# Attention, SoLU-MoE and softplus-MoE on one core: sums transposed as four columns and repeated by DMAs, the first q in two pieces, new numbers for the list schedule

## The chip, the core and the metric

The kernel runs on one core of a Trainium2 chip. The metric is the device time of one execution in microseconds (us). A core has a matrix engine (TensorE, PE in the rows; its weight loads are PEld), VectorE (DVE), ScalarE (ACT), GpSimd (POOL, hardly used here) and SyncE (SP), which issues transfers; the engines run beside each other, each in the order of its own instructions, and wait for one another by semaphores. Matrix products land in PSUM, everything else lives in SBUF; DRAM is reached by transfers (DMA).

## What is computed

```python
scores = scale * np.matmul(q, k.transpose(0, 1, 3, 2))      # 4 batches, 8 heads, 576 x 64
thresh = np.max(scores, axis=-1, keepdims=True) - tau
scores = np.where(scores >= thresh, scores, -1e9)
attn = np.exp(scores - np.max(scores, axis=-1, keepdims=True))
attn = attn / (np.sum(attn, axis=-1, keepdims=True) + 1e-09)
x = (attn @ v) -> (2304, 512)
h = x @ w_in                     # 512 x 1024
solu = h * softmax(h)
x = layernorm(solu) * g_ln @ w_out          # 1024 x 512
h = x @ w2_in                    # 512 x 2048
out = softplus(h) @ w2_out       # 2048 x 512
```

## The kernel before

Attention works on pairs of heads that lie on the upper and lower 64 partitions. A score block (L393) is four products of 128 query rows by 288 keys; its two halves fill the two score buffers in PSUM, so the next block can't start before both have been read. On each half VectorE takes the row maximum (L349), ScalarE the exponential (L350), VectorE the mask, with the row sums as a by-product (L352). TensorE then transposes the masked scores against an identity (L368), ScalarE copies the result to SBUF (L371), and TensorE multiplies by v (L429). An item is one pair of heads with one or two such query blocks; there are 36 of them, 8 with one block and 28 with two, and 8 items for the rest of 64 rows that divide by their sums in another way.

The product has the queries along its free dimension, and so the reciprocals of the sums, which come out with queries on partitions (L357, L358, a tile `rinv` of 128 x 2 or 4), have to be turned too. Before, ScalarE repeats each of the columns 64 times (`rb`, L402), TensorE transposes the 128 x 128 that this makes (L408, one for each block), ScalarE copies the outcome (`x`, L410), and VectorE multiplies the product by it (L432).

The transposed attention output goes through the first MoE in units of 256 rows (L567 to L635) and is stored to DRAM (`x2s`); from there blocks of 512 rows go through the second MoE (L678, L701). The weights come as float64 words, and VectorE and ScalarE make two parts of each, high and low (L488 to L515): this preparation of `w_in` and `w_out` falls in the start, between the first attention items. Products of four banks of PSUM, the tag `w`, are shared by everything that isn't a score block.

A planner sets the order of all of it. Every operation is entered with an engine, a duration (`occ`, `fin`), what it waits for, the buffers that it takes, and a due time from tables of numbers (`JT`, `JA`, `LO`, `LAGS`, `LD`, `JIT`, `PREP` and others). `Plan.order` is a list scheduler: it runs the durations through a model of the engines, the transfers and TensorE's clock, and takes among the operations ready on an engine the one that is due first; `AHEAD` is how many ns it lets an engine wait for one due earlier. The program then stands in the order of the modelled starts. Where the model leaves TensorE idle early on, it puts in filler products of the identity (L288).

Of the kernel before, what the change touches and what calls it, by code (L numbers as in the profile page):

```python
# [9 lines left out]
F32 = mybir.dt.float32  # L10
# [12 lines left out]
P = 128  # L23
# [56 lines left out]
WARM = 130e3  # L80

# [7 lines left out]
class Plan:  # L89
# [17 lines left out]
    def order(self):  # L107
# [12 lines left out]
        mode, dma, done = "", 0, []  # L120
        win, work, slow = 0, {}, False
# [31 lines left out]
        while any(cand.values()):  # L153
# [62 lines left out]
def tile_attention_solu_softplus(ctx: ExitStack, tc: tile.TileContext, q, k, v, tau, w_in, w_out, g_ln, w2_in, w2_out, out):  # L216
# [22 lines left out]
    done = plan_of(nc, ctx, sb, const, ident, minus, pools, stacks, w1t, x2s, q, k, v, tau, w_in, w_out, g_ln, w2_in, w2_out, out).order()  # L239
# [24 lines left out]
def plan_of(nc, ctx, sb, const, ident, minus, pools, stacks, w1t, x2s, q, k, v, tau, w_in, w_out, g_ln, w2_in, w2_out, out):  # L264
# [5 lines left out]
    plan = Plan(dict(w=W_, s=S_, h2=4, E=NE, T=2, eT=NET, x=2, xr=NXR, xrT=1, q=NPAIR, k=NPAIR, v=NPAIR, ln=3, u=2,  # L270
# [28 lines left out]
    o_minus = op("ACT", 200, 300, lambda: act.activation(out=minus, in_=ident, func=AF.Copy, scale=-1.0), after=[o_ident], due=-60)  # L299
    o_table = op("ACT", 1300, 1300, lambda: act.preload_act_table_set("natural_log_exp_and_others"), due=-49.5)  # L300

    def queue(what, i):
        return "ACT" if f"{what}{i}" in ON_ACT else "SP"

    def load_qk(p, due):
# [4 lines left out]
        z["kq"], ql = [], []  # L310
# [66 lines left out]
    def item(n):  # L377
# [4 lines left out]
        sums = buf("at", "sums", f"sums{n}", [P, 4], bufs=4)  # L382
        E = [buf("at", "E", f"E{n}_{i}", [P, 1152], bufs=NE) for i in range(nt)]
        masks = {}
        for kk, i in enumerate(ts):
# [8 lines left out]
            sc = op("PE", 970, 1128, emit_s, after=z["kq"] + [z["scaled"]], takes=s, uses=[z["q"], z["k"]], due=j + JIT[n], mode="R")  # L394
# [6 lines left out]
        rb = buf("at", "rb", f"rb{n}", [P, 4, 64])  # L401
# [459 lines left out]
```

## Time and profile before

| | |
|---|---|
| median of 3 runs | 911.1 us (910.85 to 911.49) |
| profiled execution, its own time | 914.37 us |
| its span, first to last instruction | 912.6 us |
| mean granted clock of TensorE | 0.996 |
| TensorE busy | 899.6 us of the span |
| VectorE, ScalarE busy | 690.4, 591.1 us |
| transfers | 64.63 MB, mean 71 GB/s |

The profiled execution takes 1.8 us beside its span and lies 3.3 us above the median of the other runs. Matrix products overlap in the engine's pipe, so a busy time holds a modelled end; spacings between the starts of products tell more than their mean durations.

### The profile page before, as it was taken

How to read it: one execution, taken by the hardware profiler on the slowest of the kernel's cores; microseconds unless marked ns; L12 is line 12 of the kernel's file. 1: busy time of each engine (PE TensorE's matmuls, PEld its weight loads, DVE VectorE, ACT ScalarE, POOL GpSimd, SP SyncE). 2: the span in 40 equal slices, each digit the busy share in tenths (PEclk: the TensorE clock that was granted, in tenths of full speed). 3: DMA queues.
4: the chain of work that ended last, by engine and by line, in shares of the span. 5: the costliest groups of instructions: out<-in, count | busy, mean ns of one | idle time of the engine just before them, and what ended most of it. 6: DMA issues, size and time to landing. Idle time of an engine off the chain costs nothing.

```text
span 912.6 us, 14433 instructions
## 1 busy us (share of the span) xinstructions
PE 899.6 (99%) x5458; PEld 709.6 (78%) x5458; DVE 690.4 (76%) x1474; ACT 591.1 (65%) x1159; POOL 0.7 (0%) x6
## 2 busy tenths in 40 slices
PE   8999999999999999999999999999999999999998
PEld 6576676677677677788888878888888888888897
DVE  5999898898777778599958969985556555655565
ACT  6978887997778687676757746764444444444454
POOL 0000000000000000000000000000000000000000
PEclk9999999999999999999999999999999999999999
DMA  9405110230231000164414223430021001100010
GB/s 281 161 1 175 54 30 1 84 83 24 66 109 62 2 1 12 59 219 162 139 59 162 93 98 110 135 119 24 1 92 47 1 1 47 47 0 1 1 47 24
DMA packets 32052, 64.63 MB, mean 71 GB/s; under 512 B 3440, under 2 KB 12912, under 8 KB 31984
## 3 DMA queue, kind: packets, MB, share of 16 engines
q1 hardware_dynamic: 31104, 61.62, 20.8%
q10 hardware_dynamic: 880, 2.10, 0.8%
q8 instruction: 43, 0.70, 0.3%
q14 instruction: 25, 0.20, 0.1%
HBM read 49.55 MB, written 14.16 MB: 70 GB/s over the span
## 4 chain that ended last, share of the span: by engine, by line
PE 83%; DVE 7%; ACT 4%; DMA 4%; issue 1%; SPq 1%; ACTq 0%; DVEq 0%
PE w L701 21%; PE h L678 20%; PE w L567 8%; PE w L368 7%; PE w L429 6%; PE s L393 6%; PE w L627 6%; PE w L628 3%; PE w L610 1%; PE w L472 1%; DMA raw<-in_w_in_dram 1%; DVE E L352 1%; DVE nm L349 1%; PE s L450 1%; DMA q<-in_q_dram 1%
## 5 line engine op out<-in xcount | busy, mean ns | idle before, releaser
L678 PE MATMUL h<-x2m,w2h 128*128 128x512 f32 (+1 forms) x640 | 181.6, 368 | 0.0
L678 PEld LDWEIGHTS h<-x2m,w2h 128*128 128x128 f32 x640 | 116.5, 188 | 21.0
L349 DVE TENSOR_REDUCE nm<-s 128x1 f32<-128x576 f32 x144 | 102.7, 752 | 21.7 <-PE s L393 19.1
L678 PE MATMUL h<-x2m,w2l 128*128 128x512 f32 (+1 forms) x320 | 117.7, 368 | 0.0
L701 PE MATMUL w<-wo2h,gh 128*128 128x512 f32 x288 | 112.9, 392 | 1.1 <-ACT wo2h L503 1.1
L701 PE MATMUL w<-wo2l,gh 128*128 128x512 f32 x288 | 113.0, 393 | 0.6 <-DVE wo2l L505 0.6
L352 DVE SCALAR_TENSOR_TENSOR E<-E,etau 128x576 f32<-128x576 f32 x128 | 101.1, 815 | 16.3 <-ACT E L350 14.9
L701 PE MATMUL w<-wo2h,gl 128*128 128x512 f32 x288 | 112.7, 391 | 0.0
L371 ACT COPY eT<-w 128x512 f32<-128x512 f32 (+1 forms) x188 | 92.9, 554 | 19.5 <-PE w L368 18.9
L689 ACT ACTIVATE t<-h 128x512 f32<-128x512 f32 (+1 forms) x80 | 44.3, 554 | 90.9 <-PE h L678 90.9
L627 PE MATMUL w<-lhl,wo1h 128*128 128x512 f32 x288 | 102.8, 397 | 0.0
L350 ACT ACTIVATE E<-s,nm 128x576 f32<-128x576 f32 x128 | 91.6, 756 | 11.2 <-DVE nm L349 11.0
L691 DVE TENSOR_SCALAR gw<-t 128x512 f32<-128x512 f32 (+1 forms) x80 | 31.8, 399 | 80.3 <-ACT t L690 80.1
L693 ACT ACTIVATE gw<-gw 128x512 f32<-128x512 f32 (+1 forms) x80 | 47.1, 589 | 61.1 <-DVE t L692 60.0
L393 PE MATMUL s<-k,q 64*128 64x288 f32 x512 | 83.9, 429 | 2.0 <-ACT E L350 1.4
L628 PE MATMUL w<-lhl,wo1l 128*128 128x256 f32 x288 | 80.7, 280 | 0.0
L429 PE MATMUL w<-eT,v 128*64 128x256 f32 (+1 forms) x720 | 77.8, 364 | 1.6 <-ACT eT L371 1.5
L368 PE MATMUL w<-ident,E 128*128 128x128 f32 x576 | 78.4, 279 | 0.0
L368 PEld LDWEIGHTS w<-ident,E 128*128 128x128 f32 x576 | 63.6, 141 | 17.4 <-issue 6.4
L694 DVE SCALAR_TENSOR_TENSOR gw<-h,gw 128x512 f32<-128x512 f32 (+1 forms) x80 | 51.0, 637 | 33.1 <-ACT gw L693 32.0
L429 PEld LDWEIGHTS w<-eT,v 128*64 128x64 f32 x720 | 47.1, 138 | 28.0 <-ACT eT L371 4.4
L678 PEld LDWEIGHTS h<-x2m,w2l 128*128 128x128 f32 x320 | 60.3, 188 | 10.1
(107 smaller groups left out, 1573.2 us busy)
## 6 DMA issues: line engine op xcount, KB each, us to landing
x2s<-x SPq DMA_DIRECT2D x36, 256.0 KB, 2.0
x2m<-x2s SPq DMA_DIRECT2D x18, 512.0 KB, 6.0
raw_in<-in_w_in_dram SPq DMA_DIRECT2D x16, 512.0 KB, 3.8
raw_out<-in_w_out_dram SPq DMA_DIRECT2D x16, 512.0 KB, 3.6
v<-in_v_dram SPq DMA_DIRECT2D x15, 320.0 KB, 3.4
q<-in_q_dram SPq DMA_DIRECT2D x28, 144.0 KB, 3.6
out_dram<-yo SPq DMA_DIRECT2D x15, 256.0 KB, 2.1
raw<-in_w_out_dram SPq DMA_DIRECT2D x3, 1024.0 KB, 7.8
```

Of the source, the lines that this page charges most:

```text
L349: mx = op("DVE", 668, 750, lambda: dve.tensor_reduce(out=nm.t, in_=src(), axis=AX.XY, op=ALU.max, negate=True), after=[after], takes=[nm], ...
L350: ex = op("ACT", 638, 741, lambda: act.activation(out=dst().rearrange("p (a b) -> p a b", a=2), in_=src(), func=AF.Exp, bias=nm.t, scale=1.0),
L352: return op("DVE", 739, 900, lambda: dve.scalar_tensor_tensor(out=dst(), in0=dst(), scalar=etau, in1=dst(), op0=ALU.is_ge, op1=ALU.mult, a ...
L368: pe.transpose(bk.t[:, P * i:P * i + P], b_.t[:, c:c + P], ident)
L371: copies.append(op("ACT", occ, occ + 111, lambda: act.copy(out=eT.t[:, 0:width], in_=bk.t[:, 0:width]), after=[g], uses=[bk, eT], due=due))
L393: pe.matmul(s[h].t[:, nh, 0:288], z["q"].t[r, c:c + P], z["k"].t[r, 288 * nh:288 * nh + 288], start=True, stop=True)
L429: pe.matmul(o_.t[64 * h:64 * h + 64, 0:W], z["v"].t[:, vcols(c, h)], e[8 if c == 8 else 4 * h + c](), start=(i == 0), stop=(i == 4))
L567: pe.matmul(ps.t, x__[:, part, :], w_[:, part, 512 * n:512 * n + 512], start=(part == 0 and j_ == 0), stop=(part == 3 and j_ == 2))
L627: pe.matmul(o.t.rearrange("p (a q) -> p a q", a=2), w1t["wo1h"][:, c, P * m:P * m + P], lhl.t[:, :, c, :], start=(c == 0), stop=False)
L628: pe.matmul(o.t[:, 0:256], w1t["wo1l"][:, c, P * m:P * m + P], lhl.t[:, 0, c, :], start=False, stop=(c == 7))
L678: pe.matmul(ps.t[:, 0:n], w2t["in", a, c][:, part, :], x.t[:, b_, part, 0:n], start=(part == 0 and j_ == 0), stop=(part == 3 and j_ == 2))
L701: pe.matmul(ys[j].t, g_.t[:, P * j:P * j + P], w2t["out", a, c], start=(c == 0 and i == 0), stop=(c == NC2 - 1 and i == 2))
```

## The change

The reciprocals, two or four columns of `rinv`, are transposed as they are (L412 of the new file), to 2 or 4 partitions of 128 queries. ScalarE copies these rows (`r4`, L413), a transfer writes them to a small DRAM buffer `rs`, and two further transfers read them back, each row repeated over 64 partitions, into `x`. The first pair's q is loaded and scaled in two pieces, columns 0 to 191 and the rest. The multiplication moves from L432 to L437. The durations that the planner is told of are changed in many places, its transfer model starts at 2500 ns and its clock model slow, and every table of due times has new numbers.

```diff
-JT = [0.34, 7.73, 0.9, -3.39, 0.54, 0.49, 0.42, 9.02, 0.11, 3.15, -3.13, -0.51, -5.45, 1.01, 1.21, 6.91, -4.6, 8.15, -0.49, -0.88, -1.72, -3.81, 4.75, 9.79, 2.6, 9.72, 9.11, -5.74, -0.21, 2.17, 6.22, 2.62, -2.76, -1.92, 0.89, -0.0, -0.65, 0.66, -0.91, -2.44, -7.92, -1.24, -0.04, -1.57]
+JT = [11.45, 5.07, 3.31, 9.75, -11.65, 3.47, -0.64, -1.63, -10.27, 1.59, -2.28, 3.3, 9.05, 4.22, 9.97, -7.59, 4.34, -11.96, 7.76, 0.13, 0.83, 21.82, 2.41, 10.51, 14.94, -3.8, 1.84, -8.57, 4.79, -4.06, -8.32, -0.54, 0.33, -3.15, -15.82, 8.18, 2.14, 4.06, -0.76, 0.02, -5.72, -14.29, -0.14, 3.14]
...
-AHEAD = dict(PE=0, DVE=0, ACT=0, SP=20, POOL=20, X=20)
+AHEAD = dict(PE=35, DVE=100, ACT=10, SP=500, POOL=20, X=20)
...
+FIRST = 2500
...
-        mode, dma, done = "", 0, []
-        win, work, slow = 0, {}, False
+        mode, dma, done = "", FIRST, []
+        win, work, slow = 0, {}, True
...
-                o.end = dma + 1900
+                o.end = dma + 1900 + (o.fin or 0)
...
+    rs = [dram.tile([4, P], F32, tag=f"rs{n}", name=f"rs{n}") for n in range(len(items_of()))]
...
-        for h in range(2):
-            r = slice(64 * h, 64 * h + 64)
-            ql.append(load(queue("q", p), lambda r=r: q_.t[r, :], lambda h=h: q[p][:, 640 * h:640 * h + 576], 144, takes=() if h else [q_], uses=[q_] if h else (), due=due))
-        z["scaled"] = op("ACT", 574, 678, lambda: act.activation(out=q_.t, in_=q_.t, func=AF.Copy, scale=0.125), after=ql, uses=[q_], due=due + 0.5)
+        cuts = [0, 192, S] if p == 0 else [0, S]
+        z["scaled"] = []
+        for a, e in zip(cuts, cuts[1:]):
+            ql = []
+            for h in range(2):
+                r = slice(64 * h, 64 * h + 64)
+                tk = a == h == 0
+                ql.append(load(queue("q", p) if a == 0 else "SP", lambda r=r, a=a, e=e: q_.t[r, a:e], lambda h=h, a=a, e=e: q[p][:, 640 * h + a:640 * h + e], (e - a) / 4, takes=[q_] if tk else (), uses=() if tk else [q_], due=due + (1 if a else 0)))
+            occ = 110 + 0.806 * (e - a)
+            z["scaled"].append(op("ACT", occ, occ + 104, lambda a=a, e=e: act.activation(out=q_.t[:, a:e], in_=q_.t[:, a:e], func=AF.Copy, scale=0.125), after=ql, uses=[q_], due=due + 0.5))
...
-            sc = op("PE", 970, 1128, emit_s, after=z["kq"] + [z["scaled"]], takes=s, uses=[z["q"], z["k"]], due=j + JIT[n], mode="R")
+            sc = op("PE", 970, 1128, emit_s, after=z["kq"] + z["scaled"][0:1 if i == 0 else 2], takes=s, uses=[z["q"], z["k"]], due=j + JIT[n], mode="R")
...
-        rb = buf("at", "rb", f"rb{n}", [P, 4, 64])
-        o3 = op("ACT", 187 if nt == 1 else 310, 298 if nt == 1 else 410, lambda: act.copy(out=rb.t[:, 0:w, :], in_=rv.t[:, 0:w].unsqueeze(2).to_broadcast([P, w, 64])), after=[o2], takes=[rb], uses=[rv], due=jl + D_SUM)
         rbk = bank()
+        r4 = buf("at", "r4", f"r4{n}", [4, P], bufs=2)
         x = buf("at", "x", f"x{n}", [P, 256], bufs=2)
-
-        def emit_r():
-            for i in range(nt):
-                pe.transpose(rbk.t[:, P * i:P * i + P], rb.t[:, 2 * i:2 * i + 2, :].rearrange("p a b -> p (a b)"), ident)
-        rg = op("PE", 109 * nt, 109 * nt + 163, emit_r, after=[o3, o_ident], takes=[rbk, x], uses=[rb], due=jl + D_X, mode="T")
-        xc = op("ACT", 162 if nt == 1 else 263, 270 if nt == 1 else 395, lambda: act.copy(out=x.t[:, 0:W], in_=rbk.t[:, 0:W]), after=[rg], uses=[rbk, x], due=jl + D_X)
+        rg = op("PE", 64, 227, lambda: pe.transpose(rbk.t[0:w, 0:P], rv.t[:, 0:w], ident), after=[o2, o_ident], takes=[rbk], uses=[rv], due=jl + D_X, mode="T")
+        rc = op("ACT", 160, 265, lambda: act.copy(out=r4.t[0:w, :], in_=rbk.t[0:w, 0:P]), after=[rg], takes=[r4], uses=[rbk], due=jl + D_X)
+        wr = load("SP", lambda: rs[n][0:w], lambda: r4.t[0:w, :], 1, after=[rc], uses=[r4], due=jl + D_SUM)
+        xc = [load("SP", lambda h=h: x.t[64 * h:64 * h + 64, 0:W].rearrange("p (i q) -> p i q", q=P), lambda h=h: bass.AP(tensor=rs[n].tensor, offset=rs[n].offset + P * h, ap=[[0, 64], [2 * P, nt], [1, P]]), 16 * nt, late=1800, after=[wr], takes=[x] if h == 0 else (), uses=[x] if h else (), due=jl + D_SUM) for h in range(2)]
...
-            t2.append(op("ACT", 590, 695, lambda i=i: act.activation(out=T[i].t[:, 0:576], in_=T[i].t[:, 0:576], func=AF.Copy, scale=rv.t[:, i:i + 1]), after=[t1[i]], uses=[T[i], rv], due=jl + D_SUM))
+            t2.append(op("ACT", 667, 765, lambda i=i: act.activation(out=T[i].t[:, 0:576], in_=T[i].t[:, 0:576], func=AF.Copy, scale=rv.t[:, i:i + 1]), after=[t1[i]], uses=[T[i], rv], due=jl + D_SUM))
```

Three places show what the numbers do to the order. The first is TensorE's start, from the end of the first score block on; `s` are score buffers, `rb` the repeated sums, `rinv` the plain ones, products of `ident` alone are fillers. Before:

```order
L393 MATMUL s_0_1_140<-k_107,q_101 128x288
L393 MATMUL s_0_0_139<-k_107,q_101 128x288
L288 MATMUL w_150<-ident 128x128 x11
L393 MATMUL s_0_1_181<-k_129,q_132 128x288
L393 MATMUL s_0_0_180<-k_129,q_132 128x288
L393 MATMUL s_0_1_181<-k_129,q_132 128x288
L393 MATMUL s_0_0_180<-k_129,q_132 128x288
L368 MATMUL w_195<-ident,E_0_168 128x128 x4
L408 MATMUL w_209<-ident,rb_201 128x128
L368 MATMUL w_212<-ident,E_0_168 128x128 x4
L368 MATMUL w_224<-ident,E_0_168 128x128
L393 MATMUL s_0_1_230<-k_145,q_162 128x288
```

And now:

```order
L401 MATMUL s_0_1_178<-k_151,q_145 128x288
L401 MATMUL s_0_0_177<-k_151,q_145 128x288
L290 MATMUL w_189<-ident 128x128 x10
L412 MATMUL w_224<-ident,rinv_218 2x128
L401 MATMUL s_0_1_227<-k_173,q_184 128x288
L401 MATMUL s_0_0_226<-k_173,q_184 128x288
L401 MATMUL s_0_1_227<-k_173,q_184 128x288
L401 MATMUL s_0_0_226<-k_173,q_184 128x288
L376 MATMUL w_240<-ident,E_0_205 128x128 x4
L376 MATMUL w_248<-ident,E_0_205 128x128 x4
L376 MATMUL w_257<-ident,E_0_205 128x128
L290 MATMUL w_260<-ident 128x128 x5
```

The transposition of the first item's sums now stands between the fillers and the second score block, which before followed the fillers directly, and all nine transpositions of the first masked scores follow that block without a break.

The second place is SP's queue at the start: `k`, `q` and `v` of the head pairs in the order of their issue. Before, from the second pair's k on (what stands ahead is the first pair's k and `tau`; the first q is issued by ScalarE):

```order
L295 DMA k_129<-in_k_dram 64x576
L295 DMA k_129<-in_k_dram 64x640
L295 DMA q_132<-in_q_dram 64x576 x2
L295 DMA v_137<-in_v_dram 128x640
L295 DMA k_145<-in_k_dram 64x576
L295 DMA k_145<-in_k_dram 64x640
L295 DMA q_162<-in_q_dram 64x576 x2
L295 DMA v_170<-in_v_dram 128x640
L295 DMA v_175<-in_v_dram 128x640
L295 DMA v_178<-in_v_dram 128x640
L295 DMA k_186<-in_k_dram 64x576
L295 DMA k_186<-in_k_dram 64x640
```

And now, from the second piece of the first q on:

```order
L297 DMA q_145<-in_q_dram 64x384 x2
L297 DMA v_167<-in_v_dram 128x640
L297 DMA tau_sb<-in_tau_dram 128x1
L297 DMA v_171<-in_v_dram 128x640
L297 DMA k_173<-in_k_dram 64x576
L297 DMA k_173<-in_k_dram 64x640
L297 DMA q_184<-in_q_dram 64x576 x2
```

Two v loads stand ahead of the second pair's k and q. Further down the new queue, `rs` is the store of the rows of sums, `x` the reads of them, `raw` the first weights:

```order
L297 DMA q_246<-in_q_dram 64x576 x2
L297 DMA rs_96<-r_232 2x128
L297 DMA raw_0_273<-in_w_in_dram 128x2x1024 x2
L297 DMA raw_2_0_285<-in_w_in_dram 128x1024
L297 DMA x_305<-rs_96 64x128 x2
L297 DMA raw_2_1_321<-in_w_in_dram 128x1024
L297 DMA raw_3_2_331<-in_w_in_dram 128x1024
```

The first read of sums, and the weight loads behind it, wait in SP's order for the store; 2.5 MB of weights stand between the two.

The third place is VectorE's queue from the second maximum (`nm`) of the fourth score block to the first multiplication by `x` in the new order, with the preparation of `w_in` (`raw`) between. Before, the same stretch, from the mask of the third block:

```order
L432 TENSOR_TENSOR xr_253<-w_252,x_210 128x128
L352 SCALAR_TENSOR_TENSOR E_0_268,sums_283<-E_0_268,etau 128x576 x2
L357 TENSOR_SCALAR rinv_301<-sums_283 128x2
L489 TENSOR_SCALAR raw_0_235<-raw_0_235 128x1024
L349 TENSOR_REDUCE nm_0_314<-s_0_0_294 128x1
L491 SCALAR_TENSOR_TENSOR raw_0_235<-raw_0_235 128x1024
L349 TENSOR_REDUCE nm_1_330<-s_0_1_295 128x1
L489 TENSOR_SCALAR raw_0_235<-raw_0_235 128x1024
L492 SCALAR_TENSOR_TENSOR raw_0_235<-raw_0_235 128x1024
L491 SCALAR_TENSOR_TENSOR raw_0_235<-raw_0_235 128x1024
L432 TENSOR_TENSOR xr_253<-w_349,x_273 128x128
```

And now:

```order
L357 TENSOR_REDUCE nm_1_368<-s_0_1_338 128x1
L496 SCALAR_TENSOR_TENSOR raw_0_273<-raw_0_273 128x1024
L366 RECIPROCAL rinv_345<-rinv_345 128x2
L497 SCALAR_TENSOR_TENSOR raw_0_273<-raw_0_273 128x1024
L494 TENSOR_SCALAR raw_0_273<-raw_0_273 128x1024
L494 TENSOR_SCALAR raw_2_0_285<-raw_2_0_285 128x512
L496 SCALAR_TENSOR_TENSOR raw_0_273<-raw_0_273 128x1024
L496 SCALAR_TENSOR_TENSOR raw_2_0_285<-raw_2_0_285 128x512
L497 SCALAR_TENSOR_TENSOR raw_0_273<-raw_0_273 128x1024
L497 SCALAR_TENSOR_TENSOR raw_2_0_285<-raw_2_0_285 128x512
L494 TENSOR_SCALAR raw_2_1_321<-raw_2_1_321 128x512
L437 TENSOR_TENSOR xr_294<-w_293,x_305 128x128
```

Before, the first multiplication (L432) is past at the head of this piece and the second stands in it; now the first (L437) stands at the end, behind the weights of the first two transfers.

## Rows read from the trace of the kernel before

**Rows 1.** Page, shares of the span, and two lines of the 40 slices.
```profile
PE 899.6 (99%) x5458; PEld 709.6 (78%) x5458; DVE 690.4 (76%) x1474; ACT 591.1 (65%) x1159; POOL 0.7 (0%) x6
...
DVE  5999898898777778599958969985556555655565
...
PEclk9999999999999999999999999999999999999999
```

**Rows 2.** Windows: stretch; us, then busy us (instructions) by engine, clock, DMA share, GB/s.
```profile
0.00:50.00 50.00, 44.72 (x305) 32.40 (x307) 38.64 (x87) 40.59 (x78) 0.70 (x6) 0.97 0.62 202
...
50.00:100.00 50.00, 49.00 (x411) 34.57 (x413) 47.62 (x96) 41.44 (x81) 0.00 (x0) 1.00 0.27 81
...
100.00:150.00 50.00, 49.53 (x377) 34.30 (x374) 46.92 (x122) 42.74 (x90) 0.00 (x0) 1.00 0.14 39
...
200.00:250.00 50.00, 50.00 (x381) 34.99 (x378) 41.97 (x104) 37.83 (x79) 0.00 (x0) 1.00 0.14 43
...
540.00:550.00 10.00, 8.27 (x28) 6.10 (x27) 10.00 (x20) 6.17 (x12) 0.00 (x0) 0.83 0.32 107
```

**Rows 3.** Waits of PE: total us, times, longest us.
```profile
PE w L429 <- ACT eT L371: 1.5, 1, 1.5
```

**Rows 4.** Groups of PE, then its timeline: start us, us, what, xcount.
```profile
L408 PE MATMUL w<-ident,rb 128*128 128x128 f32 x64 | 14.1, 292 | 0.5 <-ACT rb L402 0.5
...
L368 PE MATMUL w<-ident,E 128*128 128x128 f32 x576 | 78.4, 279 | 0.0
...
13.28 0.71 PE L368 MATMUL w<-ident,E 128*128 128x128 f32 x5
...
17.12 1.04 PE L368 MATMUL w<-ident,E 128*128 128x128 f32 x8
```

**Rows 5.** Groups of weight loads (PEld) by shape.
```profile
L368 PEld LDWEIGHTS w<-ident,E 128*128 128x128 f32 x576 | 63.6, 141 | 17.4 <-issue 6.4 <-ACT eT L371 4.1 <-DVE rinv L357 1.6
...
L429 PEld LDWEIGHTS w<-eT,v 128*64 128x64 f32 x720 | 47.1, 138 | 28.0 <-ACT eT L371 4.4 <-issue 4.4 <-ACT rb L402 1.0
```

**Rows 6.** Groups of ACT by shape: repeated rows and the copy of x.
```profile
L402 ACT COPY rb<-rinv 128x256 f32<-128x256 f32 x28 | 11.7, 416 | 10.6 <-DVE rinv L358 9.7 <-DVE m_t L596 0.8
...
L410 ACT COPY x<-w 128x256 f32<-128x256 f32 x28 | 10.9, 390 | 6.2 <-PE w L408 6.1
```

**Rows 7.** Timeline of the start: q scaled, score blocks, the second block's last exponential.
```profile
6.01 0.68 ACT L317 ACTIVATE q<-q 128x576 f32<-128x576 f32 x1 [0.84 <-DMA q<-in_q_dram]
...
6.74 1.31 PE L393 MATMUL s<-k,q 64*128 64x288 f32 x8 [0.47 <-ACT q L317]
...
8.77 0.68 ACT L317 ACTIVATE q<-q 128x576 f32<-128x576 f32 x1 [1.99 <-DMA q<-in_q_dram]
...
10.63 1.37 PE L393 MATMUL s<-k,q 64*128 64x288 f32 x8
...
13.74 0.75 ACT L350 ACTIVATE E<-s,nm 128x576 f32<-128x576 f32 x1
...
13.91 1.87 PE L393 MATMUL s<-k,q 64*128 64x288 f32 x8
...
18.59 1.87 PE L393 MATMUL s<-k,q 64*128 64x288 f32 x8 [0.43 <-ACT E L350]
```

**Rows 8.** Groups of DVE by shape: maxima and masks.
```profile
L349 DVE TENSOR_REDUCE nm<-s 128x1 f32<-128x576 f32 x144 | 102.7, 752 | 21.7 <-PE s L393 19.1 <-PE s L450 2.1
...
L352 DVE SCALAR_TENSOR_TENSOR E<-E,etau 128x576 f32<-128x576 f32 x128 | 101.1, 815 | 16.3 <-ACT E L350 14.9
```

**Rows 9.** Transfers: page, then 0 to 40 us; KB each, median us to landing.
```profile
x2s<-x SPq DMA_DIRECT2D x36, 256.0 KB, 2.0
...
DMA packets 3812, 10.08 MB, mean 252 GB/s; under 512 B 736, under 2 KB 736, under 8 KB 3808
...
raw<-in_w_in_dram SPq DMA_DIRECT2D x4, 512.0 KB, 10.8
...
g_sb<-in_g_ln_dram SPq DMA_DIRECT2D x1, 4.0 KB, 5.0
```

More of the change, by code (lines that the diff above doesn't have):

```diff
@@ L290, in plan_of, with load @@
     plan.filler = filler
-    def load(eng, out, in_, kb, after=(), takes=(), uses=(), due=0.0):
+    def load(eng, out, in_, kb, after=(), takes=(), uses=(), due=0.0, late=0):
         e = sp if eng == "SP" else act
-        return op(eng, 620, None, lambda: e.dma_start(out=out(), in_=in_()), after=after, takes=takes, uses=uses, due=due, kb=kb)
+        return op(eng, 620, late, lambda: e.dma_start(out=out(), in_=in_()), after=after, takes=takes, uses=uses, due=due, kb=kb)
     st = {}
     o_ident = op("POOL", 500, 700, lambda: make_identity(nc, ident), due=-100)
-    o_minus = op("ACT", 200, 300, lambda: act.activation(out=minus, in_=ident, func=AF.Copy, scale=-1.0), after=[o_ident], due=-60)
-    o_table = op("ACT", 1300, 1300, lambda: act.preload_act_table_set("natural_log_exp_and_others"), due=-49.5)
+    o_minus = op("ACT", 200, 300, lambda: act.activation(out=minus, in_=ident, func=AF.Copy, scale=-1.0), after=[o_ident], due=-5)
+    o_table = op("ACT", 1300, 1300, lambda: act.preload_act_table_set("natural_log_exp_and_others"), due=-80)
     def queue(what, i):
@@ L381, in item @@
         W = P * nt
-        sums = buf("at", "sums", f"sums{n}", [P, 4], bufs=4)
+        sums = buf("at", "sums", f"sums{n}", [P, 4], bufs=8)
         E = [buf("at", "E", f"E{n}_{i}", [P, 1152], bufs=NE) for i in range(nt)]
@@ L450, in emit_s @@
                         pe.matmul(s[i].t[o:o + 64, nh, 0:288], zs[i]["q"].t[r, c:c + 64], zs[i]["k"].t[r, kc:kc + 288], start=True, stop=True)
-        sc = op("PE", 970, 1128, emit_s, after=[a for z in zs for a in z["kq"] + [z["scaled"]]], takes=s, uses=[z[a] for z in zs for a in "qk"], due=j + JIT[n], mode="Q")
+        sc = op("PE", 970, 1128, emit_s, after=[a for z in zs for a in z["kq"] + z["scaled"]], takes=s, uses=[z[a] for z in zs for a in "qk"], due=j + JIT[n], mode="Q")
         scores.append(sc)
-        sums = buf("at", "sums", f"sums{n}", [P, 4], bufs=4)
+        sums = buf("at", "sums", f"sums{n}", [P, 4], bufs=8)
         T = [buf("at", "T", f"T{n}_{i}", [P, 640], bufs=2) for i in range(2)]
@@ L487, in convert @@
         w_ = lambda: lw().bitcast(F32)
-        a1 = op("ACT", 100 + 950 * k_, 200 + 960 * k_, lambda: act.activation(out=hw().bitcast(F32), in_=hw().bitcast(F32), func=AF.Copy, scale=2.0 ** -112), after=after, uses=[raw], due=due - 0.1)
+        a1 = op("ACT", 69 + 1022 * k_, 181 + 1008 * k_, lambda: act.activation(out=hw().bitcast(F32), in_=hw().bitcast(F32), func=AF.Copy, scale=2.0 ** -112), after=after, uses=[raw], due=due - 0.1)
         a2 = op("DVE", 70 + 535 * k_, 150 + 540 * k_, lambda: dve.tensor_scalar(out=lw(), in0=lw(), scalar1=29, scalar2=None, op0=ALU.logical_shift_right), after=after, uses=[raw], due=due)
@@ L499, in convert @@
             for i in range(2):
-                h = op("ACT", 525, 620, lambda i=i: act.activation(out=hi()[:, i, :], in_=w_()[:, i, :], func=AF.Copy, scale=scale(i)), after=[a4, o_g], uses=[raw], due=due)
-                low.append(op("DVE", 602, 692, lambda i=i: dve.scalar_tensor_tensor(out=lo()[:, i, :], in0=w_()[:, i, :], scalar=scale(i), in1=f(hi()[:, i, :]), op0=ALU.mult, op1=ALU.subtract), after=[h], uses=[raw], due=due))
+                h = op("ACT", 666, 794, lambda i=i: act.activation(out=hi()[:, i, :], in_=w_()[:, i, :], func=AF.Copy, scale=scale(i)), after=[a4, o_g], uses=[raw], due=due)
+                low.append(op("DVE", 665, 752, lambda i=i: dve.scalar_tensor_tensor(out=lo()[:, i, :], in0=w_()[:, i, :], scalar=scale(i), in1=f(hi()[:, i, :]), op0=ALU.mult, op1=ALU.subtract), after=[h], uses=[raw], due=due))
             return low
-        a5 = op("ACT", 100 + 850 * k_, 200 + 850 * k_, lambda: act.copy(out=hi(), in_=w_()), after=[last], uses=[raw], due=due)
+        a5 = op("ACT", 68 + 1004 * k_, 158 + 1018 * k_, lambda: act.copy(out=hi(), in_=w_()), after=[last], uses=[raw], due=due)
         if not turned:
```

44 lines of the change are left out of this document (22 added, 22 removed).

## The prediction

> **What bounds the kernel now.** I read the page's shares first. TensorE counts as busy for 899.6 of 912.6 us, at nearly full clock in every slice [rows 1], so the time is TensorE's work plus the little it stands still. The table by stretch shows where that is [rows 2]: 5.3 us of the first 50 us idle, 1.0 of the next 50, 0.5 of the third, nothing at 200 to 250, and 1.7 of 10 us at 540 with the clock down to 0.83. In the first 50 us a part of the busy time is L288's filler, which computes nothing, so the start loses more than 5.3. VectorE is busy for 47.6 and 46.9 us of the two stretches of 50 us from 50 on, for 42.0 at 200 [rows 2]: up to about 150 us it is as full as TensorE. The longest single wait behind ScalarE is 1.5 us [rows 3]. So a change can take TensorE work away, shorten the start, or lose by a new wait; ScalarE work alone buys little.
>
> **Step 1, the transposed sums.** 64 transpositions of 128 repeated columns (L408) go. Their spacing: eight transpositions show as 1.04 us and five as 0.71, so one more costs 0.11 [rows 4]; the 292 ns of their group is a duration that overlaps the next. Gone: 64 x 0.11 = 7.0 us. Added: one transposition per group of tiles, 36, whose stationary operand is 2 or 4 columns wide while the identity's 128 columns still stream. No row has such a step. From above it is 0.11, from below nothing. Weight loads with 64 columns take 138 ns, with 128 columns 141 [rows 5], so the nearest row shows no gain from a narrow operand. I take 0.08, nearer to the row than to nothing, since this one is 32 times narrower, not twice: 36 x 0.08 = 2.9. Step 1 is -4.1 us, with bounds -3.1 (0.11 each) and -7.0 (0 each). It counts in full only where TensorE is the limit.
>
> The Trainium skill, TensorE: Matmul & The Clock Gate, section LDWEIGHTS, says that a weight load takes time in proportion to the columns loaded. By that rule the load of 4 columns all but vanishes and streaming alone is left. The 138 against 141 ns do not agree with it, though they are durations and not spacings. By the row step 1 is -3.1; by the rule it would be about -5, an estimate with half a step left for streaming.
>
> **Step 2, the order.** TensorE's kinds of matmul alternate 283 times in the new order, 277 in the old. A switch has no row of its own; I price it at one transposition step, 6 x 0.11 = +0.6 us, with bounds 0 and +1.2. The 29 fillers become 25; they only fill waits, so nothing.
>
> **Step 3, ScalarE.** The 36 repeats (L402) go, 28 of them at 416 ns, and the copies of 128 x 256 (390 ns, L410) become copies of 2 or 4 rows [rows 6]. That is over 11.7 us off an engine that was not the limit. Worth 0; VectorE's and TensorE's work covers it. At most it takes back the 1.5 us wait of [rows 3]. Corrected durations in the list change no instruction; they act through the order alone.
>
> **Step 4, the start.** Before: the whole first q is scaled from 6.01, for 0.68 us; score blocks start at 6.74, 10.63, 13.91 and 18.59 [rows 7]. Now the first block needs a third of q. Scaling shortens by 0 to 0.45 us and the smaller load lands 0 to 1 us earlier, so the first block gains between 0 and 1.4; I take 1.1, and it starts at 5.6. Then the gain is lost. In SP's new order two v loads of 320 KB stand ahead of the second k and q. At the 252 GB/s of this stretch [rows 9] they take 2.5 us of the queue, so the second q, scaled from 8.77 before, is ready about 2 to 2.5 later, and with 0.68 of scaling the second block starts at 11.5 to 12.0 instead of 10.63. The third cannot start before the second's exponentials have emptied both score buffers: before, these ended at 14.49, 3.86 after the block's start, which makes 15.4 to 15.9 instead of 13.91. The fourth, 4.7 behind the third as before, falls at 20.1 to 20.6 or, if only exponentials hold it, 19.3: +0.7 to +2.0. I carry +1.3. Then VectorE limits: its order puts fifteen passes over w_in between the maxima of the fourth block and its masks (fourteen before), and every block costs it two maxima of 0.75 and two masks of 0.82 us [rows 8], of which the change removes none; with next to no idle time until 150 us it can't catch up there. Behind 200 us it has 16% free, and attention is spread wider (its last product moves from TensorE row 1690 to 1915 of 3810), so part of the lag comes back. I keep +0.8 of the +1.3; bounds -1 (the lost time of the start shrinks) and +3 (all is kept and VectorE's fuller queue adds as much again).
>
> **Step 5, the round trip.** Each group now has a store of 1 or 2 KB to DRAM and two reads. A 256 KB store lands in 2.0 us, a 4 KB load in the crowded start in 5.0, a 512 KB load there in 10.8 [rows 9]. With a copy of 0.4 at most, a trip takes 5 to 8 us, against 0.8 for repeat and copy before [rows 6]. What waits is the multiplication L432 (now L437) on VectorE, which needs the attention product too; behind it stand the next maxima and masks, and then TensorE's next blocks; it also holds one of four banks. In most groups the product comes several microseconds after the sums anyway, and the list puts the multiplication behind other VectorE work. I price it at 0, with bounds 0 and +5.4 (0.15 us for each of 36).
>
> SP issues 108 more transfers and waits in order for each store; the loads queued behind are small or early. From the last unit of the first MoE on, the order repeats the old one: 27 matmuls of h, 24 of y, the same preparation. The loss at 540 stays.
>
> **Sum.** -4.1 + 0.6 + 0.8 = -2.7 us on the profiled execution's own 914.4 (span 912.6, 1.8 around it): 911.7. That execution lies 3.3 over the runs' median of 911.1, so I forecast 908.4. Differences under 0.2%, 1.8 us, a measurement of this kernel can't tell from no change.
>
> **Rivals.**
> *The round trip decides (slower).* Price 0.15 us a group, 5.4, and with it the first bound of step 1 and a lag of 2: 911.1 - 3.1 + 0.6 + 2 + 5.4 = 916; already 0.125 us a group (4.5) turns my sum into a loss of 1.8. For it: the first read stands behind 2.5 MB of w_in in SP's order, and VectorE has no slack up to 150 us. Against: later the rings are nearly empty, and sums precede products. The Trainium skill, DMA: Bandwidth & Descriptors, section Rules for kernel authors, says transfers under 64 KB pay mostly overhead. The trace agrees, with 2.0 us even for 256 KB unloaded and 5.0 for 4 KB. Chance 0.22.
> *The start eats the gain (no change).* Lag of 3 instead of 0.8: 908.4 + 2.2 = 910.6. For it: the two v loads and 95% VectorE. Against: the free 16% later. Chance 0.25.
> *The new order fits better.* Idle time of 50 to 150 us and half of the start's goes, 1.5 + 2.6: 908.4 - 4.1 = 904.3. For it: only there is anything to win. Against: the two v loads, and VectorE, from which nothing is removed. Chance 0.13.
> *My forecast,* 905.5 to 909.3: chance 0.40.
>
> Faster by over 0.2% (under 909.3) are the forecast and the better order, 0.53; within 0.2%, 0.25; slower, 0.22. The range runs from 903 (a little under the better order, with a cheaper narrow step) to 914.5, which cuts off the worse part of the round trip's case; some 0.15 stay outside.
>
> **What would show it.** Step 1: the new transposition's spacing, 0.08 or 0.11, and 36 of them. Step 4: score blocks at 5.6, 11.5 to 12, 15.4 to 15.9, 19.3 to 20.6. Step 5: VectorE's idle time before the multiplication with a DMA of x as releaser; over 4 us in all and the rival holds. I am wrong if VectorE's share from 20 to 150 us falls (the start fits better), if TensorE waits for x or a bank held by it, or if stillness between 200 and 527 us, nearly none today, grows past 2 us.

## The result and the profile after

| | before | after |
|---|---|---|
| median, 4 runs each | 911.05 us (910.85 to 911.49) | 919.91 us (918.28 to 921.26) |
| ratio | | 1.0096 [1.0078, 1.0113] |
| span of the profiled execution | 912.6 us | 916.5 us |
| mean granted clock in it | 0.996 | 0.993 |

The change costs 8.9 us (7.1 to 10.3 by the interval); the prediction was a gain of 2.7 with an upper end of 914.5. Four executions of the runs below, three of the kernel before and one of v_behind, took 1262 to 2269 us and are left out of medians and ratios. The profiled executions differ by less than the medians (914.4 against 918.3), since the one of before lies 3.3 above its median and the one of after 1.6 below.

The page after (compare [rows 1]) and the table by stretch ([rows 2]), with columns as there:

```profile
PE 898.1 (98%) x5422; PEld 705.5 (77%) x5422; DVE 694.9 (76%) x1474; ACT 578.5 (63%) x1123; POOL 0.7 (0%) x6
```

```profile
0.00:50.00 50.00, 42.58 (x257) 29.26 (x258) 34.55 (x70) 34.79 (x63) 0.70 (x6) 0.90 0.66 207
50.00:100.00 50.00, 46.89 (x386) 33.17 (x386) 46.24 (x102) 38.77 (x75) 0.00 (x0) 1.00 0.30 91
100.00:150.00 50.00, 50.00 (x400) 34.44 (x400) 46.27 (x114) 40.06 (x81) 0.00 (x0) 1.00 0.19 54
...
540.00:550.00 10.00, 9.34 (x40) 7.23 (x39) 6.96 (x13) 4.16 (x7) 0.00 (x0) 1.00 0.32 109
```

TensorE is busy for 2.1 us less in the first 50 us and 2.1 less in the next 50 than before, and the clock of the first stretch falls from 0.97 to 0.90. At 540 the change has won 1.1 us, but from 500 to 550 as a whole TensorE stands still for 2.35 us, against 1.73 before. Most of the loss is made in the first 100 us. TensorE's waits after (engine, buffer, line, releaser; total us, times, longest):

```profile
PE w L517 <- ACT r L413: 2.1, 1, 2.1
PE w L615 <- DVE h L603: 1.7, 2, 1.2
PE s L401 <- ACT q L325: 1.6, 1, 1.6
...
PE w L412 <- DVE rinv L366: 1.2, 1, 1.2
PE w L376 <- DVE xr L437: 1.2, 1, 1.2
PE w L376 <- ACT eT L379: 1.0, 1, 1.0
```

And where they lie, in TensorE's timeline (start, us, what; idle before it in brackets), to be held against [rows 7]:

```profile
5.07 2.09 PE L401 MATMUL s<-k,q 64*128 64x288 f32 x8
7.09 2.50 PE L290 MATMUL w<-ident 128*128 128x128 f32 x20
10.80 0.27 PE L412 MATMUL w<-ident,rinv 128*2 128x128 f32 x1 [1.21 <-DVE rinv L366]
12.67 1.51 PE L401 MATMUL s<-k,q 64*128 64x288 f32 x8 [1.60 <-ACT q L325]
...
17.77 1.24 PE L401 MATMUL s<-k,q 64*128 64x288 f32 x8
...
20.18 0.27 PE L412 MATMUL w<-ident,rinv 128*2 128x128 f32 x1
20.29 1.04 PE L376 MATMUL w<-ident,E 128*128 128x128 f32 x8
21.25 1.28 PE L401 MATMUL s<-k,q 64*128 64x288 f32 x8
...
24.64 0.33 PE L376 MATMUL w<-ident,E 128*128 128x128 f32 x1 [0.97 <-ACT eT L379]
24.90 1.77 PE L401 MATMUL s<-k,q 64*128 64x288 f32 x8
26.59 0.27 PE L412 MATMUL w<-ident,rinv 128*2 128x128 f32 x1
28.96 2.08 PE L517 MATMUL w<-raw,ident 128*128 128x512 f32 x2 [2.09 <-ACT r L413]
...
43.42 1.24 PE L401 MATMUL s<-k,q 64*128 64x288 f32 x8
```

The fillers, which before ran right up to the second score block, now end before the first transposition of sums; TensorE stands still for 1.21 us ahead of that and for 1.60 behind it, the second time until ScalarE has scaled the second pair's q. At 24.64 and 28.96 it waits for a bank of PSUM. The copies that free these two stand on ScalarE among the preparation of `w_in`:

```profile
22.25 1.16 ACT L493 ACTIVATE raw<-raw 128x1024 f32<-128x1024 f32 x1
23.37 0.74 ACT L358 ACTIVATE E<-s,nm 128x576 f32<-128x576 f32 x1
24.01 0.58 ACT L379 COPY eT<-w 128x512 f32<-128x512 f32 x1
...
25.74 1.23 ACT L493 ACTIVATE raw<-raw 128x1024 f32<-128x1024 f32 x1
27.03 1.15 ACT L508 CAST w1h<-raw 128x1024 fp32r<-128x1024 f32 x1
28.08 0.70 ACT L493 ACTIVATE raw<-raw 128x512 f32<-128x512 f32 x1
28.67 0.24 ACT L413 COPY r<-w 2x128 f32<-2x128 f32 x1
```

TensorE's clock by stretch (from, to; length, busy, granted clock):

```profile
7.00:13.60 6.60, 3.78 (x31) 1.00 1.02 259
13.70:17.00 3.30, 3.30 (x17) 0.50 1.07 280
17.10:27.30 10.20, 8.80 (x71) 1.00 1.03 375
27.40:34.10 6.70, 5.14 (x12) 0.50 0.22 80
34.20:40.00 5.80, 5.80 (x34) 1.00 0.27 73
```

In two stretches the granted clock is 0.50, the lower of its two levels, 1.2 GHz against 2.4. Both come after waits: 2.8 us of idle time lie between 9.6 and 12.7, and 3.1 between 23.7 and 29. The 8.4 us that the engine was busy at half clock do the work of 4.2.

### The profile page after: what moved, and what is told of

The parts are those of the page before. It is cut to its first block, busy times and chain, and to the rows that moved or that the text cites. A ratio compares the mean times of both kernels' runs of the same rounds, so it can differ in the third digit from the quotient of the medians.

```text
span 916.5 us, 14566 instructions
## 1 busy us (share of the span) xinstructions
PE 898.1 (98%) x5422; PEld 705.5 (77%) x5422; DVE 694.9 (76%) x1474; ACT 578.5 (63%) x1123; POOL 0.7 (0%) x6
## 4 chain that ended last, share of the span: by engine, by line
PE 85%; DVE 5%; DMA 4%; ACT 3%; issue 2%; SPq 1%; ACTq 0%; DVEq 0%
PE w L706 21%; PE h L683 20%; PE w L572 8%; PE w L376 8%; PE s L401 8%; PE w L434 7%; PE w L632 5%; PE w L633 3%; DMA raw_in<-in_w_in_dram 2%; PE w L615 1%; PE w L477 1%; SPq L297 1%; PE w L517 1%; DMA raw<-in_w_out_dram 1%; DMA q<-in_q_dram 1%
## 5 line engine op out<-in xcount | busy, mean ns | idle before, releaser
L701 ACT CAST gh<-gw 128x512 fp32r<-128x512 f32 (+1 forms) x80 | 46.2, 578 | 82.2 <-PE w L706 69.5
L702 DVE TENSOR_TENSOR gl<-gw,gh 128x512 fp32r<-128x512 f32 (+1 forms) x80 | 50.9, 636 | 32.2 <-ACT gh L701 32.2
```

## The experiments

Ratios are to the kernel before, run on the same chip in the same turn; its medians there lie between 911.8 and 913.2 us, 1 to 2 above the 911.05 of the result, so that differences of this size between two turns say little. Lines in rows are those of the kernel named.

### The changed kernel with one suspect taken away

**v_behind** issues the first two loads of v behind the second pair's k and q on SP. **no_trip** fills `x` from the input k, so that nothing waits for the store:

```diff
+    last = max(a.start for a in plan.st[1]["scaled"][0].after)   # v_behind
+    for p in range(2):
+        plan.st[p]["vl"].start = last + 0.1 * (p + 1)
-bass.AP(tensor=rs[n].tensor, offset=rs[n].offset + P * h, ap=[[0, 64], [2 * P, nt], [1, P]])
+bass.AP(tensor=k.tensor, offset=k.offset + P * h, ap=[[0, 64], [2 * P, nt], [1, P]])   # no_trip
```

> The changed kernel with every engine's order kept, but the first two v loads moved in SP's queue behind the second pair's k and q. Theory A (the loss is made in the start: the second score block starts at 12.67 us instead of 10.63 because two v loads stand ahead of its q, banks are held, and TensorE's clock falls to half for it): second block at 11 to 11.5, the stretch at half clock at 13.7 us gone, 2 to 4 us faster than the changed kernel's 919.9, so 916 to 918. Theory B (the round trip of the sums through DRAM costs the time, wherever it is): nothing changes, 919 to 921.

> The changed kernel with the order kept and all its transfers, but the repeated rows are read from the input k instead of from the stored sums, so that no read waits for a store (the output is divided by wrong numbers). Theory A: at most 1.5 us faster, 918 to 920, since the multiplications wait for VectorE's own queue and not for x. Theory B: 5 us or more faster, 915 or less, and SP issues the weights of the start earlier.

v_behind: 919.75 us, 1.0076 [1.0051, 1.0101]; no_trip: 919.80, 1.0072 [1.0050, 1.0095], inside its theory A. Neither is the cause by itself. With v behind, the second block did start at 10.7 us again, but the third waits 3.3 us and the fifth starts at 27.7 instead of 24.9; the mean clock is 0.70 from 17.1 to 34.1 us. The loss only moves. **before_again**, the kernel before as it is, gives the spread of a measurement: 913.14 (911.21 to 917.84), 1.0011 [0.9990, 1.0032]. Its profiled execution took 911.47 us. The stretch from 45.6 to 49.0 us, which ran at a clock of 0.50 in the earlier profile of the same kernel, runs at 1.00 in it, behind the same wait of 1.00 us. So part of the 3.3 us by which that earlier execution lies over its median is the clock.

> The kernel before, once more, to see what its profiled execution of 914.4 us had that its timed runs of 911 had not. Both theories: ratio 1.000 within 0.002. If the start's luck with the clock makes the difference, a profile near 911 shows the stretch at half clock (before: 45.6 to 49.0 us) gone or elsewhere, and about 2 to 3 us less on the way to 60 us; if it is the profiler, the profile repeats 914.

**banks_early** moves two copies forward on ScalarE. **fillers** puts 20 products of the identity, which compute nothing, into free columns of banks that are held anyway: 7 behind the first transposition of sums, 4 ahead of the wait at 24.64, 9 ahead of that at 28.96. **both** does the two, **fill_first** the copies and the first 7 alone.

```diff
+    for i, o in enumerate((it[1]["copies"][-1], it[2]["copies"][-1])):
+        o.start = raw1.start - 2 + i            # banks_early
+    fill(it[0]["rg"], 7, it[0]["bank"], False)  # fillers
+    fill(it[2]["copies"][-1].after[0], 4, it[0]["out"], True)
+    fill(it[2]["rg"], 9, it[0]["out"], False)
```

> The changed kernel with its order kept, except that on ScalarE the last copies of the second and third group's transposed exponentials come ahead of the second scaling of w_in's first pieces, so that two PSUM banks come free about 1 to 2.5 us earlier. Theory A (TensorE is held by banks in the stretch where w_in is prepared): the wait of 2.1 us at 28.96 is gone or under 0.5, the later half-clock stretch is shorter, and the time is 916 to 918 us, 2 to 4 under the changed kernel. Theory S (the late score blocks, held by VectorE, decide): the wait goes to another place, block six still starts at 42 to 44 us, and the time is 919 to 921.

> The changed kernel with its order kept and 20 matmuls added that compute nothing, into free columns of banks already held, at the three waits of the first 30 us, so that TensorE does not stand still there. Theory C (the fall of TensorE's clock to half after those waits is the cost): no row of half clock at 13.7 to 17.1 and 27.3 to 34.1 us, and 3 to 5 us faster than the changed kernel, 915 to 917 us. Theory A or S (the waits themselves, the clock being only their companion): 918.5 to 921 us, even where the clock stays full.

> The changed kernel with its order kept, the two copies earlier and the 20 idle matmuls added. If banks and clock each cost their part: 913 to 916 us. If only one of them does, the time of that one alone. If neither does and the late score blocks decide (theory S): 919 to 921 us.

> The changed kernel in its order with the two copies moved ahead of the second scaling of w_in, and only the 7 idle matmuls at the first wait. If the first wait alone brings the clock down once the banks come free earlier: clock at full from 10 us on and 912.5 to 914.5 us. If the later waits bring it down too: 915 to 918, a half-clock stretch between 20 and 40 us.

| | median us | ratio | block six starts |
|---|---|---|---|
| banks_early | 917.52 | 1.0056 [1.0038, 1.0074] | 42.5 |
| fillers | 914.73 | 1.0036 [1.0023, 1.0049] | 41.0 |
| both | 914.99 | 1.0034 [1.0021, 1.0047] | 40.8 |
| fill_first | 915.35 | 1.0038 [1.0022, 1.0053] | 40.5 |

None of the four came out at the 919 to 921 of theory S; fill_first had the full clock of its first theory to 60 us and, at 0.9 over that range, the time of its second. The same stretches in fillers, and two rows of its timeline:

```profile
13.70:17.00 3.30, 3.30 (x27) 1.00 1.06 271
17.10:27.30 10.20, 10.06 (x78) 1.00 1.02 368
27.40:34.10 6.70, 6.56 (x43) 1.00 0.25 93
...
24.80 1.77 PE L412 MATMUL s<-k,q 64*128 64x288 f32 x8
...
28.91 1.17 PE L529 MATMUL w<-raw,ident 128*128 128x512 f32 x2
```

Idle products at the waits keep the clock up and give back 5 to 5.5 us (1.0096 to 1.0036, with an interval of 2 us either way), though they do no work and what stands behind the waits starts no earlier (24.80 and 28.91, against 24.90 and 28.96). The first half-clock stretch therefore cost nothing that lasts. The second did: the sixth block comes 2.4 us earlier without it. The rest of the gain comes later; 1.4 us of it is stillness between 450 and 550 us (2.96 us in the changed kernel, 1.54 in fillers), and why that shrinks isn't shown. Freeing the banks earlier gives back 2.4 to 3.6 by itself, with the second of the half-clock stretches gone (1.00 from 27.4 to 34.1 us), and nothing more once the clock holds. What is left is 3 us over the kernel before. By the pages TensorE stands still for 13.4 us in fillers and for 12.7 in before_again, and is busy for 898.9 (idle products included) and 897.0: the idle products take the place of the waits, at full clock, and the new order's start stays longer. In all four the sixth score block starts at 40.5 to 42.5 us, 34.9 in before_again.

### The parts in the order of the kernel before

**path_old** makes the new path of the sums at the old places, **q_old** the two pieces of q, **path_q_old** both:

```diff
-            for i in range(nt):
-                pe.transpose(rbk.t[:, P * i:P * i + P], rb.t[:, 2 * i:2 * i + 2, :].rearrange("p a b -> p (a b)"), ident)
+            pe.transpose(rbk.t[0:w, 0:P], rv.t[:, 0:w], ident)
-lambda: act.copy(out=x.t[:, 0:W], in_=rbk.t[:, 0:W])
+            act.copy(out=r4.t[0:w, :], in_=rbk.t[0:w, 0:P])
+            sp.dma_start(out=rs[n][0:w], in_=r4.t[0:w, :])
+            for h in range(2):
+                sp.dma_start(out=x.t[64 * h:64 * h + 64, 0:W]..., in_=bass.AP(tensor=rs[n].tensor, ...))
```

> The kernel before with its order kept and only the path of the sums changed: at the old places one transposition of 2 or 4 columns, one copy of 2 or 4 rows, the store and the two reads of x; no repeats, no wide transpositions. Theory N (the path gains and the new order loses): 907 to 909.5 us, 2 to 4 under the kernel before, whose work it shortens by 3.1. Theory P (the path costs by itself, by waits for x or for banks): 911 us or more, with waits of TensorE or VectorE behind the reads.

> The kernel before with its order kept and only the first q loaded and scaled in two pieces, the second piece on SP behind the first k. The first score block starts at 5 to 5.6 us instead of 6.7 to 7.5. If the start's lead is kept: 909.5 to 910.5 us. If the next blocks, which wait for the second q, stand where they stood: no change, 911 to 912.

> Both parts in the order of the kernel before. Theory N: 906 to 909 us, the sum of the two parts, faster than both kernels. Theory P: 911 or more.

path_old took 959.01 us, 1.0494 [1.0470, 1.0518]; path_q_old 959.52, 1.0525 [1.0499, 1.0550]; q_old 916.29, 1.0037 [1.0019, 1.0054]. The first two fall under their theory P, far beyond its 911; q_old misses both of its expectations. By its trace q_old loses because two more transfers on SP push the later ones back: the fourth pair's q is scaled at 20.13 us instead of 18.37, and the fourth block starts at 21.5 instead of 19.7, while the first starts no earlier than 7.2, since the old order has fillers ahead of it. Of path_old, **path_early** moves the copy right behind the transposition, and **path_early_pool** issues the transfers from GpSimd too; **both_pool** does that in the new order:

```diff
+    for rg, xc in plan.trips:
+        xc.start = rg.start + 300               # path_early
-            sp.dma_start(out=rs[n][0:w], ...)
+            pool.dma_start(out=rs[n][0:w], ...) # path_early_pool
```

> As path_old, the order before with the new path of the sums, but the copy of the sums' rows stands on ScalarE right behind their transposition (0.3 us later in the list's time), so that store and reads start sooner. If the place of the copy made the trip late: VectorE's wait for x falls from 29 us to under 8 and the time is 912 to 925. If the trip is too long even then: over 930 us.

> As path_early, and store and reads are issued by GpSimd, which has nothing else to do, so that SP's loads stand behind no store. If SP's waits hold back loads: faster than path_early by 3 us or more. If the path gains its 3.1 us once nobody waits for it: 907 to 912 us in all. If it still stands over 915, the trip itself is what the old order can't hide.

> The changed kernel in its order, with the two earlier copies and the idle matmuls of the run before, and the store and the reads of x issued by GpSimd instead of SP. If SP's waits for the copies hold loads back in the new order too: 910 to 913 us. If they hold back nothing that is needed: 914 to 916, as without.

path_early took 959.60 us, 1.0531 [1.0511, 1.0551]; path_early_pool 966.83, 1.0603 [1.0588, 1.0617]; both_pool 915.10, 1.0031 [1.0021, 1.0042]. Neither an earlier copy nor GpSimd's queue helps. VectorE's waits in path_early show what is common to them:

```profile
DVE xr L446 <- DMA x<-rs: 34.5, 11, 6.8
```

The row copy and the multiplication that needs it, in path_early:

```profile
44.21 0.26 ACT L417 COPY r<-w 2x128 f32<-2x128 f32 x1
...
52.18 0.29 DVE L446 TENSOR_TENSOR xr<-w,x 128x128 f32<-128x128 f32 x1 [6.76 <-DMA x<-rs]
```

The third item in the kernel before, where `x` needs no trip:

```profile
34.77 0.35 ACT L410 COPY x<-w 128x128 f32<-128x128 f32 x1
...
35.47 0.30 DVE L432 TENSOR_TENSOR xr<-w,x 128x128 f32<-128x128 f32 x1
```

The fourth item in the changed kernel:

```profile
43.49 0.25 ACT L413 COPY r<-w 2x128 f32<-2x128 f32 x1
...
51.73 0.28 DVE L437 TENSOR_TENSOR xr<-w,x 128x128 f32<-128x128 f32 x1
```

Over the 36 items, the time from the end of the row copy to the multiplication is under 5 us in 13 before (35.47 - 35.12 = 0.35 here), and never under 7.2 after. At the eleven places of path_early where VectorE waits for `x`, this distance is the trip's time: 4.3 to 7.7 us (52.18 - 44.47 = 7.7 here) in nine of them, 9.9 and 12.6 in the other two. The old order has no room for it; the new one has, for every item.

**fixed_old** and **fixed_new** take the trip out of the two orders, **fixed_old_trip** only the waiting for it:

```diff
-dve.tensor_tensor(out=xt..., in0=o_.t[:, 0:W], in1=x.t[:, 0:W], op=ALU.mult)
+dve.tensor_tensor(out=xt..., in0=o_.t[:, 0:W], in1=z["v"].t[:, 0:W], op=ALU.mult)
```

> The kernel before with its order kept: transpositions of 2 or 4 columns and copies of their rows as in the changed kernel, but store and reads are left out and the multiplication takes a fixed tile (v) in place of x, so the products aren't divided by their sums. If the path is worth what its work says (step 1, 3.1 us of TensorE, and ScalarE's repeats): 907 to 909.5 us, 2.5 to 5 under the kernel before. If TensorE's saving is eaten by the start's waits anyway: 911 to 913.

> As fixed_old, but the store and the two reads of x are issued at their places; nobody waits for x. If the wait for x was the whole cost of the path in the old order: within 1 us of fixed_old. If SP's waits for the copies, which hold back the loads behind them, cost too: 3 us or more above it.

> The changed kernel with its order kept; store and reads are left out and the multiplication takes a fixed tile (v) in place of x, as in fixed_old, so that the same work stands in the two orders. If the order alone costs (theory of the start: banks, first waits, clock): 918 to 920.5 us, 10 to 12 over fixed_old, and the same waits of TensorE at 12.7, 24.6 and 29.0 us. If the transfers still cost something in the new order: 911 to 917.

| | median us | ratio | span, mean clock in the profile |
|---|---|---|---|
| fixed_old | 908.14 | 0.9950 [0.9931, 0.9968] | 905.8, 1.000 |
| fixed_old_trip | 931.41 | 1.0187 [1.0160, 1.0214] | 935.0, 0.987 |
| fixed_new | 917.39 | 1.0053 [1.0035, 1.0072] | 914.8, 0.996 |

The pages of before_again, fixed_old and fixed_new, in this order:

```profile
PE 897.0 (99%) x5458; PEld 707.8 (78%) x5458; DVE 689.7 (76%) x1474; ACT 590.6 (65%) x1159; POOL 0.7 (0%) x6
...
PE 893.9 (99%) x5430; PEld 702.6 (78%) x5430; DVE 688.8 (76%) x1474; ACT 576.7 (64%) x1123; POOL 0.7 (0%) x6
...
PE 897.1 (98%) x5422; PEld 704.6 (77%) x5422; DVE 694.6 (76%) x1474; ACT 578.6 (63%) x1123; POOL 0.7 (0%) x6
```

The path's work is worth 4.5 us where nobody waits for its rows; 3.1 of them are TensorE's busy time (897.0 to 893.9, both at full clock). The same work in the new order takes 9.0 us more in the profiles: TensorE is busy for 3.2 more, with a mean clock of 0.93 in the first 50 us where fixed_old has 1.00, and stands still for 5.8 more (17.7 against 11.9). Of this stillness 2.7 lie in the first 50 us, 1.6 in the next 50 and 1.7 between 500 and 550 us. The transfers alone cost the old order 22 to 23 us, without anyone reading their result, since SP waits in order. Of path_old's 50 us over fixed_old (1.0494 - 0.9950) the other 28 come close to the 29.2 us that VectorE waits for `x` there. SP's own waits in fixed_old_trip:

```profile
SPq L414 <- ACT r L413: 114.5, 25, 14.6
...
SPq L416 <- DMA rs<-r: 52.4, 36, 8.9
```

So the first `w_in` comes later; ScalarE sits on it, and TensorE on a copy behind that:

```profile
25.32 1.18 ACT L496 ACTIVATE raw<-raw 128x1024 f32<-128x1024 f32 x1 [5.01 <-DMA raw<-in_w_in_dram]
...
28.30 4.54 PE L437 MATMUL w<-eT,v 128*64 128x128 f32 x40 [6.55 <-ACT eT L372]
```

In fixed_old that scaling starts at 20.89. In the new order, with the clock held by idle products, the queue costs nothing (both_pool against both: 1.0031, 1.0034). fixed_new fell between its two expectations. Its waits at 12.6, 24.7 and 29.1 us are those of the changed kernel, of the same length, and yet it is 0.43% quicker, some 4 us. Its mean granted clock was 0.992 to 0.996 in 7 runs (middle 0.996), that of the changed kernel 0.991 to 0.993: 0.003 to 0.004 of 917 us are 2.8 to 3.7, an estimate. So most of the transfers' share may go with the clock; why the clock falls for longer with them stays open. Nor is its size sure: no_trip, which has all the transfers, stands only 1.7 us over fixed_new (1.0072 against 1.0053).

**old_tables** and **old_path** cross the halves: the new code with the old tables, whose list makes a third order, and the old path (one `rb` buffer) at the places of the new order.

> The changed code (sums transposed as columns, rows repeated by transfers, first q in two pieces, corrected durations) with the tables and look-ahead numbers of the kernel before; the list makes another order from them. Theory N (the new tables' order is what costs): the start goes back to about the times of before (second block near 10.7, fifth before 30 us, little or no half-clock stretch) and the time is 908 to 912 us, the path itself being worth -3. Theory P (path, pieces or durations cost by themselves): 916 us or more, with waits of TensorE or VectorE behind the copies or the reads of x.

> The changed kernel with the order of its list kept, but the sums go the old way at the same places: ScalarE repeats the columns just ahead of the transposition, 64 transpositions of 128 columns, ScalarE copies x; no store, no reads. Theory A: the start's loss stays and the transpositions come back, 28 x 0.11 = 3.1 us on TensorE and some ScalarE work, so 921 to 924. Theory B: the round trip is gone, 4 us or more faster than 919.9, 916 or less.

932.29 us, 1.0225 [1.0208, 1.0243], under theory P, and 945.91, 1.0351 [1.0321, 1.0382], outside both. The new code loses in each order that was run. old_path says little: TensorE waits 21.6 us for `rb`, of which it has one buffer. No version of the whole computation came in under the kernel before.

## Why the prediction was wrong

Put together from the ratios, of 912 us: the path's work -4.5 (fixed_old), the order +9.4 (1.0053 - 0.9950), the transfers +3.9 (1.0096 - 1.0053); in all +8.8. They add up to the measured loss by the way they are formed. Each has an interval of about 2 us either way, and the order's share holds the two pieces of q and the numbers of buffers too.

**Step 4, the start, failed.** I had the lag at +0.8 with +3 as its end. It forecast score blocks at 5.6, 11.5 to 12, 15.4 to 15.9 and 19.3 to 20.6; they started at 5.07, 12.67, 17.77 and 21.25, and the sixth at 43.42. The step took VectorE for the only limit of the start and counted no wait of TensorE for banks held by ScalarE's copies, and it priced waits at their length alone: without the half clock that follows them the kernel is 5 us faster. In fixed_new against fixed_old, 2.7 us of stillness and the lower clock fall in the first 50 us; the 1.7 at 500 to 550 stood in no step. The rows for the clock were there: [rows 2] gives 0.97 and 0.83 for stretches with waits, though the 0.97 is the half clock at 45.6, which the second profile of that kernel didn't have. And the diff's first piece of order showed the fillers losing their cover over the second block's wait.

**Step 5, the round trip.** The price of 0 held for waits: in the new order VectorE waits before L437 for TensorE's product alone. But "In most groups the product comes several microseconds after the sums anyway" left out the 13 of 36 items with under 5 us in the order that I had the trace of, and I didn't ask what an order that makes it right for all would cost. That is what the +9.4 contain, so far as the order was made for the trip; how much of it another set of tables would save isn't shown. The rival of the round trip, 916, came nearest, by another mechanism than the runs show.

**Step 1** had the right mechanism and was mis-sized. The new transposition is followed by the next after 0.11 us (20.18 to 20.29), as a wide one: -3.1, its first bound, not -4.1, which TensorE's busy time in fixed_old bears out (897.0 to 893.9). Its weight load did shrink (compare [rows 5]; weight loads by shape):

```profile
L412 PEld LDWEIGHTS w<-ident,rinv 128*4 128x4 f32 x28 | 2.3, 82 | 6.5 <-issue 2.5 <-ACT eT L379 1.2 <-DVE E L360 0.8
```

The Trainium skill, TensorE: Matmul & The Clock Gate, section LDWEIGHTS, has the load in proportion to its columns. 82 ns for 4 against 141 for 128 goes down, but far from in proportion, and none of it shows in the spacing.

**Step 3**, 0 with at most 1.5, fits: fixed_old gains 4.5, with an interval of 2.9 to 6.3, against the 3.1 of step 1. **Step 2** as priced, 0.6 for switches of kind, wasn't measured apart. Of the signs that I named, VectorE's share from 20 to 150 us did fall, from 95% to 92%, but the start fitted worse and not better: in that stretch VectorE waited 3.1 us for score blocks, against 1.2 before. TensorE's longest wait, 2.1 us at 28.96, is for a bank that the new row copy frees, one of the signs for step 5. Stillness between 200 and 527 us grew past 2: the waits of L615 behind VectorE are 1.7 at 514 and 516 and 0.5 at 486. The loss at 540, which I had as unchanged, shrank by 1.1, less than these waits added.

## What to carry to other kernels

A round trip through DRAM is free only where the order leaves more than its time, here 4.3 to 7.7 us and more where its queue is held up, between the producer and the reader, at every place; count the places in the trace of the old order, and price the order that makes the room, not the trip alone. In a kernel that one matrix engine bounds, a wait of one or two microseconds in the start may cost its length again through the clock, and products that compute nothing are then worth their place. A transfer in an in-order queue that waits for a late producer holds back every load behind it: look at what these loads feed.

## What the runs showed of the hardware

Twenty idle products made a kernel 5 us faster, though what stands behind the waits started no earlier. The granted clock fell to 0.50 after idle stretches of 1.2 and 1.6 us close together. After a wait of 1.00 us it fell to 0.50 in one profile of the kernel before and stayed at 1.00 in another. That kernel ran between 909.2 and 917.8 us at mean clocks of 0.994 to 1.000. A store of 1 or 2 KB with two reads of 32 or 64 KB took 4.3 to 7.7 us from copy to use at nine of the eleven places where it was waited for, and issued by GpSimd it was not shorter: VectorE's wait grew from 34.5 to 54.4 us.
